# 32 stores of an intermediate tensor issued from GpSimd's queue instead of SyncE's, with a new instruction order

## The chip, the cores and the metric

The kernel runs on one NeuronCore of a Trainium2 chip. The core has TensorE (PE: matrix products, with the weight loads listed apart as PEld), VectorE (DVE), ScalarE (ACT), GpSimd (POOL) and SyncE (SP, which here issues DMA transfers). Each engine works through its own queue in order, and semaphores order the engines among each other. The metric is device time in microseconds (us); lower is better.

## The reference: three layers in a row

All tensors are float32. Batch is 4, sequence 448, model width 768.

```python
scores = cap * tanh(q @ k.T / sqrt(64) / cap)          # 12 heads of 64, per batch
x      = softmax(scores) @ v                            # layer 1: attention
h      = relu(x @ w_in)                                 # layer 2: 768 -> 1024 ("inner layer")
gate   = sigmoid(conv3(h, conv_w))                      # 3 taps along the sequence, per channel
x      = (h * gate) @ w_out                             # 1024 -> 768
for e in range(4):                                      # layer 3: 4 causal attention experts
    ye = softmax(mask(x @ wq[e] @ (x @ wk[e]).T / 8)) @ (x @ wv[e]) @ wo[e]
    out += w[e] * ye                                    # w: top-2 gate of x @ w_gate
```

## The kernel before

**Work.** The kernel folds `w_out` into the projections of layer 3 (`fold_w`, `fold_mm`), so layer 2 ends with the 8 blocks g = h * gate of 128 channels by 448 positions for each batch b. Products of float32 precision are made as three products of split operands. The stages overlap: attention of batch b + 1 runs while the inner layer of batch b is computed (`f_unit`), then come the fold, and layer 3 batch by batch.

**The values of the inner layer.** `f_unit(b, f, ...)` (L874) makes one block: matmuls into a PSUM bank, then a relu by ACT or DVE into h, which comes from the ring HT of 2 buffers. Where f < EARLY_N[b], with EARLY_N = (0, 4, 8, 0), the convolution and the gate follow at once (`conv_gate`, L898) into a buffer of the ring CT, also 2 buffers; otherwise h itself is stored and the gate is made later. The block is then stored to the DRAM tensor g_dram (L896), 224 KB at a time, 32 stores in all: 12 from CT (four of batch 1 and all eight of batch 2) and 20 from HT. `prep_g` and `prep_x` load the blocks back when layer 3 of that batch needs them. A store must have landed before its ring buffer is written again, and before its block is loaded.

**Order.** `chain_kernel` adds 2,487 operations to a `Plan`, which numbers them. They are then issued in the sequence of the tuple ORDER, written out in the source, so that each engine's queue follows it:

```python
for n in ORDER:
    for call in self.ops[n].calls:
        call()
```

The set SWAP names operations (copies, scalings, relus, absolute values) that run on the other one of ACT and DVE than the code says by default (`one_of`, L293). Each `add` states a cost, and HOP states a time between engines ("dma" 1500 ns plus size, "pool" 150 ns); no code here makes ORDER or SWAP out of them, they stand in the file as numbers.

**DMA.** Every transfer is issued by SP at L390 with a stated cost of 470 ns. POOL does memsets and selects only (L404); most stand at the start.

Of the kernel before, what the change touches and what calls it, by code (L numbers as in the profile page):

```python
# [201 lines left out]
class Plan:  # L202
# [192 lines left out]
    def store(self, out, in_, **kw):  # L395
        self.dma(out, in_, sb_in=in_, size=128 * self.cols(in_) * 4, **kw)
# [67 lines left out]
def chain_kernel(tc, first, kq, v, w_in, conv_w, woT, wqkv, wo, out):  # L464
    nc = tc.nc
    pl = Plan(nc)
# [5 lines left out]
    g_dram = tc.dram_tile([B, 128, NF, S], F32, name="g_dram")  # L472
# [401 lines left out]
    def f_unit(b, f, part, n, ring, pos, lag):  # L874
# [16 lines left out]
        g = h[:, 1:S + 1]  # L891
        if f < EARLY_N[b]:
            g = CT.next()
# [613 lines left out]
```

## Time and profile before

| | |
|---|---|
| time, median of 3 runs | 517.42 us (517.18 to 517.43) |
| the profiled execution's own time | 515.46 us |
| its span, first to last instruction | 513.8 us |
| outside the span | 1.66 us |
| TensorE clock granted in the span | 1.00, so 2.4 GHz |
| PE / DVE / ACT / POOL busy | 505.6 / 455.7 / 383.7 / 10.7 us |
| stores to g_dram | issued from 73.6 to 277.4 us |

"Busy" is the time in which an engine executes at least one instruction. The profiled execution is 1.96 us shorter than the median of the runs, so sums are made against 515.46 us and carried over to the median as differences.

### The profile page before, as it was taken

Reading aid. Unit: us, or ns where it says so; the run is one execution under the profiler, and the core shown is the slowest. Engines: PE = TensorE matmul, PEld = TensorE weight load, DVE = VectorE, ACT = ScalarE, POOL = GpSimd, SP = SyncE. Lnnn points to the kernel's source line nnn. Section 1 sums busy time; section 2 is a strip of 40 time slices with the busy share of each in tenths; the row PEclk is TensorE's granted clock in tenths of the full one; section 3 lists DMA queues with packets and bytes.
Section 4 is the critical chain, followed back from the end, with each engine's and each line's share of the span. In section 5 each row is a group of like instructions: output and inputs, shape, how many; then the busy total and the mean of one; then the engine's idle time right before and its main releaser. Section 6 shows DMA issues by size and latency. Waiting matters only on the chain.

```text
span 513.8 us, 9272 instructions
## 1 busy us (share of the span) xinstructions
PE 505.6 (98%) x3248; PEld 401.6 (78%) x3248; DVE 455.7 (89%) x1071; ACT 383.7 (75%) x689; POOL 10.7 (2%) x64
## 2 busy tenths in 40 slices
PE   9999999999999999999999999999999999999997
PEld 6344597555675576879999999999998998899886
DVE  5999999989998899798989999979879998997863
ACT  7999958999999989548534765577877777757771
POOL 4000000000000000010000000001000000000000
PEclk9999999999999999999999999999999999999999
DMA  6635346337531721465566251143577358507964
GB/s 211 194 133 184 129 155 201 122 112 185 159 104 46 199 93 62 153 200 171 187 219 203 75 169 39 54 132 92 169 232 260 115 198 273 175 20 248 307 231 153
DMA packets 48830, 81.73 MB, mean 159 GB/s; under 512 B 7696, under 2 KB 32272, under 8 KB 48784
## 3 DMA queue, kind: packets, MB, share of 16 engines
q1 hardware_dynamic: 48784, 81.15, 50.3%
q8 instruction: 25, 0.41, 0.4%
q14 instruction: 21, 0.17, 0.1%
HBM read 54.54 MB, written 22.66 MB: 150 GB/s over the span
## 4 chain that ended last, share of the span: by engine, by line
PE 68%; DVE 18%; ACT 6%; DMA 4%; issue 3%; SPq 1%; DVEq 0%; ACTq 0%
PE ps L381 67%; DVE fm L323 12%; DVE rm L323 5%; ACT fm L315 5%; SPq L390 1%; DMA fm<-p_dram 1%; DMA fm<-woT 1%; DMA p_dram<-fm 1%; DMA fm<-kq 1%; ACT rm L315 1%; DMA g_dram<-fm 0%; PE ps L385 0%; DVE ps L323 0%; DVEq L323 0%; ACTq L315 0%
## 5 line engine op out<-in xcount | busy, mean ns | idle before, releaser
L381 PE MATMUL ps<-rm 128*128 128x448 f32 (+8 forms) x2280 | 391.8, 350 | 2.8 <-ACT fm L315 2.1
L381 PEld LDWEIGHTS ps<-rm 128*128 128x128 f32 (+1 forms) x2280 | 351.6, 187 | 44.8 <-ACT fm L315 10.2
L315 ACT ACTIVATE fm<-fm 128x448 f32<-128x448 f32 (+9 forms) x233 | 168.3, 751 | 41.8 <-DVE fm L323 27.5
L323 DVE SCALAR_TENSOR_TENSOR fm<-fm 128x448 f32<-128x448 f32 (+4 forms) x240 | 147.4, 632 | 10.4 <-ACT fm L315 7.6
L315 ACT ACTIVATE fm<-ps,fm 128x896 f32<-128x896 f32 (+4 forms) x142 | 110.3, 796 | 16.6 <-DVE fm L323 7.2
L381 PE MATMUL ps<-fm 128*64 128x448 f32 (+10 forms) x952 | 115.8, 444 | 2.3 <-DVE fm L583 1.1
L381 PEld LDWEIGHTS ps<-fm 128*64 128x64 f32 (+4 forms) x952 | 48.2, 135 | 63.9 <-issue 41.3
L323 DVE TENSOR_TENSOR rm<-fm,rm 128x448 fp32r<-128x448 f32 (+4 forms) x154 | 86.7, 583 | 4.3 <-ACT rm L315 3.2
L323 DVE TENSOR_TENSOR fm<-fm 64x448 f32<-64x448 f32 (+6 forms) x112 | 61.3, 551 | 3.9 <-ACT fm L315 1.7
L315 ACT ACTIVATE fm<-ps 128x448 f32<-128x448 f32 (+5 forms) x80 | 38.6, 491 | 29.0 <-PE ps L381 25.7
L315 ACT ACTIVATE rm<-fm 128x448 fp32r<-128x448 f32 (+6 forms) x78 | 41.7, 551 | 19.6 <-DVE fm L323 15.4
L323 DVE TENSOR_SCALAR fm<-fm 128x256 int32<-128x256 int32 (+11 forms) x127 | 38.8, 322 | 6.4 <-ACT fm L315 2.8
L315 ACT ACTIVATE rm<-ps 128x386 fp32r<-128x386 f32 (+3 forms) x49 | 20.2, 424 | 19.0 <-PE ps L381 18.8
L323 DVE CAST rm<-fm 128x384 fp32r<-128x384 f32 (+6 forms) x81 | 28.8, 366 | 1.6 <-DMA fm<-kq 0.6
L315 ACT ACTIVATE rm<-rm 64x448 fp32r<-64x448 f32 (+3 forms) x50 | 24.6, 506 | 0.6
L323 DVE COPY fm<-ps 128x448 f32<-128x448 f32 (+4 forms) x27 | 13.5, 516 | 9.3 <-PE ps L381 5.6
L323 DVE TENSOR_TENSOR rm<-ps,rm 128x386 fp32r<-128x386 f32 (+1 forms) x32 | 18.7, 586 | 2.6 <-ACT rm L315 2.3
L323 DVE STREAM_TRANSPOSE fm<-fm 128x512 f32<-128x512 f32 x28 | 18.5, 692 | 1.6 <-ACT fm L315 1.4
L323 DVE TENSOR_REDUCE fm<-ps 128x1 f32<-128x384 f32 (+1 forms) x24 | 13.8, 576 | 0.4
L350 DVE CUSTOM_DVE_ANT_0 ps<-ps,fm 128x256 f32<-128x256 f32 (+1 forms) x32 | 11.3, 363 | 1.2 <-PE ps L381 0.9
L404 POOL MEMSET fm<- 64x3 f32 (+12 forms) x44 | 5.3, 148 | 324.4 <-PE ps L381 214.8
L323 DVE TENSOR_TENSOR fm<-fm,rm 128x448 f32<-128x448 f32 x18 | 11.0, 619 | 0.4 <-ACT fm L315 0.2
(27 smaller groups left out, 76.0 us busy)
## 6 DMA issues: line engine op xcount, KB each, us to landing
g_dram<-fm SPq DMA_DIRECT2D x32, 224.0 KB, 2.7
fm<-g_dram SPq DMA_DIRECT2D x32, 224.0 KB, 2.9
p_dram<-fm SPq DMA_DIRECT2D x14, 512.0 KB, 3.4
fm<-p_dram SPq DMA_DIRECT2D x28, 256.0 KB, 4.5
fm<-w_in SPq DMA_DIRECT2D x24, 256.0 KB, 2.7
fm<-woT SPq DMA_DIRECT2D x16, 384.0 KB, 3.4
fm<-kq SPq DMA_DIRECT2D x23, 256.0 KB, 3.4
out<-fm SPq DMA_DIRECT2D x23, 224.0 KB, 2.1
```

Of the source, the lines that this page charges most:

```text
L315: return self.add("act", cost, [lambda: self.nc.scalar.activation(out, in_, func, **kw)], [out] + more, [in_] + ptr)
L323: return self.add("dve", cost, [lambda: f(out, *ins, **kw)], [out], aps)
L350: self.add("dve", cost, [lambda: self.nc.vector.tensor_tensor_reduce(x, x, mask, -1.0, 3.0e38, OP.add, OP.min, least)], [x, least], [x, mask])
L381: self.nc.tensor.matmul(out, a, b, start=start, stop=stop, **kw))
L390: self.add("dma", 470.0, [lambda: self.nc.sync.dma_start(out, in_)], outs, ins, size=size, **kw)
L404: self.add("pool", cost, [lambda: f(out, *ins, **kw)], [out], [x for x in list(ins) + [kw.get("in_")] if hasattr(x, "ap")])
```

## The change

The store of each block is added by a new function, which lets GpSimd issue the transfer and states a cost of 3000 ns on POOL; the size is not stated. All other transfers stay on SP.

```diff
+    def store_by_pool(self, out, in_, **kw):
+        self.add("pool", 3000.0, [lambda: self.nc.gpsimd.dma_start(out, in_)], [], [in_], **kw)
...
-        pl.store(g_dram[b, :, f], g, keys_out=[("g", b, f)])
+        pl.store_by_pool(g_dram[b, :, f], g, keys_out=[("g", b, f)])
...
 ORDER = tuple(map(int, '''
...
-118 173 142 184 204 110 129 193 206 174 111 144 194 157 207 180 177 112 232 47 217 176 252 316 233 210 253 113 181 145
...
 SWAP = frozenset(map(int, '''
-82 86 95 99 102 110 114 124 128 133 137 144 148 151 159 166 175 186 197 204 219 223 226 230 235 250 253 265 272 278
...
+64 82 86 95 99 102 110 114 124 128 133 137 144 148 151 159 166 175 186 201 204 219 223 226 230 235 250 253 265 272 288
```

ORDER and SWAP are new. Counted through the numbered operations: the first 135 of the 2,487 places of ORDER are as before. PE's 420 operations move by 1.2 places in PE's queue on average and by 11 at most. SWAP differs in 185 numbers, which put 100 operations from ACT to DVE and 85 from DVE to ACT. In POOL's queue four older operations, memsets and a select that make masks, now stand among the stores.

## Rows read from the trace of the kernel before

**Rows 1.** The page, first part: busy us, share of the span, instructions.

```profile
PE 505.6 (98%) x3248; PEld 401.6 (78%) x3248; DVE 455.7 (89%) x1071; ACT 383.7 (75%) x689; POOL 10.7 (2%) x64
```

**Rows 2.** Busy time by stretch (--windows): PE, PEld, DVE, ACT, POOL, clock, DMA.

```profile
64.00:128.00 64.00, 63.84 (x429) 41.57 (x431) 60.39 (x121) 55.36 (x72) 0.00 (x0) 1.00 0.52 156
128.00:192.00 64.00, 64.00 (x442) 41.54 (x436) 58.28 (x99) 59.06 (x70) 0.00 (x0) 1.00 0.42 121
192.00:256.00 64.00, 64.00 (x363) 51.00 (x360) 56.19 (x95) 42.00 (x66) 1.58 (x3) 1.00 0.49 152
256.00:320.00 64.00, 64.00 (x352) 62.70 (x351) 59.09 (x123) 34.10 (x69) 0.52 (x2) 1.00 0.46 145
```

**Rows 3.** The page's chain that ended last: shares by engine.

```profile
PE 68%; DVE 18%; ACT 6%; DMA 4%; issue 3%; SPq 1%; DVEq 0%; ACTq 0%
```

**Rows 4.** What SP's queue waited for, whole span: total us, times, longest.

```profile
SPq L390 <- DVE fm L323: 164.3, 72, 12.9
SPq L390 <- DVE rm L323: 66.8, 32, 8.8
SPq L390 <- PE ps L381: 62.0, 17, 12.2
SPq L390 <- ACT fm L315: 28.8, 24, 4.6
```

**Rows 5.** g_dram's transfers (--tile): issue ns min/median/max, then landing of all.

```profile
L390 SPq DMA_DIRECT2D g_dram<-fm x32: 319/330/597, 73.6 to 277.4; - x32
...
DMA to landing us min/median/max: 1.9/2.8/6.9
```

**Rows 6.** Waits that ended in 64 to 256 us: total us, times, longest.

```profile
PEld ps L381 <- ACT fm L315: 10.0, 25, 0.8
...
PEld ps L381 <- DVE fm L323: 4.9, 12, 0.7
...
ACT fm L315 <- DMA g_dram<-fm: 2.7, 3, 1.9
...
PEld ps L381 <- DVE rm L323: 1.7, 3, 0.7
PEld ps L381 <- ACT rm L315: 1.0, 2, 0.7
ACT rm L315 <- DMA fm<-wqkv: 1.2, 1, 1.2
ACT fm L315 <- DMA fm<-w_in: 0.8, 1, 0.8
DVE rm L323 <- DMA fm<-kq: 0.6, 1, 0.6
```

**Rows 7.** Timeline of SP and of ACT about one store: start us, us, engine.

```profile
245.26 0.33 SPq L390 DMA_DIRECT2D g_dram<-fm  x1
...
247.29 0.67 ACT L315 ACTIVATE fm<-fm 128x448 f32<-128x448 f32 x1 [1.89 <-DMA g_dram<-fm]
```

**Rows 8.** Groups of DVE by form, 64 to 280 us: count, busy us, mean ns.

```profile
L323 DVE TENSOR_TENSOR rm<-fm,rm 128x448 fp32r<-128x448 f32 x37 | 22.2, 619 | 0.2
...
L323 DVE CAST rm<-fm 128x448 fp32r<-128x448 f32 x19 | 7.3, 383 | 0.9 <-DMA fm<-kq 0.6 <-PE ps L381 0.3
...
L323 DVE COPY fm<-ps 128x448 f32<-128x448 f32 x6 | 3.6, 622 | 1.3 <-PE ps L381 1.3
```

**Rows 9.** Timeline of POOL and DVE about 222 us.

```profile
221.54 0.56 DVE L323 CAST rm<-fm 128x772 fp32r<-128x772 f32 x1
...
221.76 0.49 POOL L404 MEMSET fm<- 128x128 f32 x1 [214.80 <-PE ps L381]
...
222.31 0.94 POOL L404 TENSOR_SCALAR_AFFINE_SELECT fm<-fm 128x128 f32<-128x128 f32 x1
...
223.21 0.20 POOL L404 MEMSET fm<- 128x128 f32 x1
```

**Rows 10.** Groups of ACT by form, whole span: count, busy us, mean ns.

```profile
L315 ACT ACTIVATE fm<-ps 128x448 f32<-128x448 f32 x60 | 32.0, 540 | 24.8 <-PE ps L381 22.1 <-DVE fm L323 1.6 <-PE ps L385 0.4
L315 ACT ACTIVATE rm<-fm 128x448 fp32r<-128x448 f32 x42 | 23.4, 571 | 6.5 <-DVE fm L323 3.6 <-PE ps L381 2.9
```

205 rows, old and new, of tables (ORDER, SWAP) are left out of this document.

## The prediction

> **What bounds the kernel now.** I read the page's first part first. PE is busy for 505.6 of 513.8 us, DVE for 455.7, ACT for 383.7 and POOL for 10.7 [rows 1]. The reader is to see that only PE has almost no idle time, and that POOL has nearly all of its time free. Then I cut the span into stretches [rows 2]. The stores are issued from 73.6 to 277.4 us [rows 5], which is inside these four stretches. In each of them PE is busy for 63.84 to 64.00 of 64 us; in the last PEld is busy for 62.70 as well, so there the weight loads follow each other without a break. In the stretches from 64 to 256 PEld is busy for 41.5 to 51.0 only, so there the matmuls are sometimes held up by their operands although PE counts as busy. From 64 to 256 DVE works 60.39 + 58.28 + 56.19 = 174.9 of 192 us (91%) and ACT 55.36 + 59.06 + 42.00 = 156.4 (81%).
>
> The chain that ended last says the same: PE has 68% of it, DVE 18%, ACT 6%, all DMA together 4%, and SP's queue 1% [rows 3]. SP spends its time waiting: its four longest items alone sum to 164.3 + 66.8 + 62.0 + 28.8 = 321.9 us, all of them waits for compute engines that must first make or free something [rows 4]. So SP has spare issue time; the question is only whether its order delays something that others need.
>
> Who needs it is in the waits that ended from 64 to 256 us [rows 6]. Loads that came late cost ACT 1.2 + 0.8 us and DVE 0.6 us, and no matmul or weight load names a DMA among its releasers there. The landing of a store to g_dram, which frees the buffer, cost ACT 2.7 us in 3 waits. PE's weight loads waited for ACT 10.0 + 1.0 us in 27 waits and for DVE 4.9 + 1.7 us in 15 waits.
>
> **The change, part by part.**
>
> *SP loses 32 issues.* Each takes 0.33 us [rows 5], together 10.6 us, which lie beside the 321.9 us of waiting [rows 4]. What SP can also lose is blocking: a store at the head of its queue waits for ACT or DVE, and the loads behind it wait too. The loads that come late in the stretch cost 1.2 + 0.8 + 0.6 = 2.6 us on ACT and DVE [rows 6]. Bounds: 0 to -2.6 us. I take 0, because PE names no DMA in that list and PE sets the time. If the cover goes, it is a late load of weights or of the next pair of heads that shows, on DVE first.
>
> The Trainium skill (DMA: Bandwidth & Descriptors, "Issuing engines are not separate DMA queues") says that several issuing engines share the same 16 DMA engines, and that using more of them saves sequencer time alone. By it nothing but the 10.6 us of SP's time would change, and the time would stay; that is the rival "hidden anyway" below. The trace agrees as far as SP's time is spare.
>
> *POOL gains 32 issues.* No row shows a DMA issued by POOL. The nearest rows are POOL's own instructions over 128 partitions: 0.20 us for a memset and 0.94 us for a select [rows 9]. SP's 0.33 us is the lower bound. I take 0.94 us, the longer row, so as not to underrate what I cannot see. 32 times 0.94 is 30 us in the 204 us of the stores, so POOL has room.
>
> *What waits behind a store on POOL.* In order, a store that waits for its relu or gate holds up the stores behind it and the four mask operations. In the trace of before these four run on POOL from 221.76 us on or later [rows 9], and their readers come still later, in layer 3; so nobody waits for them. A store that is held up keeps its ring buffer occupied, and the next relu or gate waits.
>
> *Landing.* Transfers of g_dram land 1.9 to 6.9 us after issue, 2.8 in the median [rows 5]. A landing that is later by 0.94 - 0.33 = 0.6 us matters only where the buffer is written again at once. Pairing each store with the next operation on its buffer, 7 of the 32 buffers are rewritten within 0.6 us of the landing. One pair shows it: the store is issued at 245.26, and ACT, idle for 1.89 us, starts at 247.29 [rows 7]. So ACT and DVE lose at most 7 x 0.6 = 4.2 us together. Six of the seven lie after 192 us, where ACT is busy for 42.0 and 34.1 of 64 us and PE never idles [rows 2]. Bounds 0 and +4.2; I take +0.3, half of the one early case. If the cover goes, PE waits for a bank that a late relu has not read. The blocks themselves are loaded back tens of us later, so no load waits.
>
> *VectorE beside POOL.* Copies, casts and scalings of DVE from SBUF to SBUF take 383 ns for 448 columns, against 619 ns for a two-operand operation and 622 for a copy from PSUM [rows 8]. There are 73 such fast ones from 64 to 280 us. One of them shows POOL suffering: the memset of 128 x 128 that ran over the cast at 221.54 took 0.49 us, the same memset at 223.21, beside none, 0.20 [rows 9]. If the exclusion also works the other way, DVE waits for POOL. 73 fast operations in 216 us start 0.32 times in the 0.94 us of a store; 32 x 0.32 = 10 meetings at half of 0.94 us each give DVE 4.8 us more. Of the 42 waits of weight loads that ACT or DVE ended, 15 were ended by DVE [rows 6]; by that share 4.8 x 15 / 42 = 1.7 us reach PE. Bounds 0 (POOL alone waits) and +4.8 (all of it reaches PE). I take +1.7, because DVE is at 91% and feeds ACT as well.
>
> The Trainium skill (SBUF — State Buffer, "SBUF: two separate sides") states such an exclusion: GpSimd and a DVE operation in a two-port mode lock each other out of a shared port pair, and transfers issued from GpSimd need it to write their descriptors. It speaks against this change. The slow memset agrees with one direction of it; no row shows the other, nor a descriptor being written.
>
> *The new order and the new shares of ACT and DVE.* PE's own order hardly moves (1.2 places on average), and the number of its instructions stays. From 64 to 256 us SWAP puts 7 PSUM reads and 21 SBUF operations of a few hundred columns from ACT to DVE, and 4 and 13 back: net 3 x 0.62 + 8 x 0.38 = 4.9 us more on DVE [rows 8] and 3 x 0.54 + 8 x 0.57 = 6.2 us less on ACT [rows 10]. DVE would be busy for 179.8 of 192 us (94%), ACT for 150.2 (78%). Weighted by who ends PE's waits [rows 6], relief of ACT could give up to 6.2 x 27 / 42 = 4.0 us, and load on DVE take up to all 4.9. I take 0: the relief goes to the engine with more room, the load to the one with less, but PE waits more often for ACT. Smaller moves within the order can't be priced from rows, and I leave them inside these bounds.
>
> *Sum.* 0 + 0.3 + 1.7 + 0 = +2.0 us: 515.46 becomes 517.5 for the profiled execution, and the median 517.42 becomes 519.4 us (+0.4%).
>
> **The rivals.**
>
> *Faster: ACT's relief reaches PE.* PE's weight loads wait for ACT 11.0 us in the stretch and for DVE 6.6 [rows 6]. If the shift of work removes 4.0 us of the first, and DVE adds only the 1.7 us of my sum, the time is 517.42 - 4.0 + 1.7 = 515.1 us. Against it: DVE at 94%. It decides if the waits for ACT fall under 9 us while those for DVE stay under 8.
>
> *Hidden anyway.* Stores are off PE's path, landings are covered, DVE and POOL don't meet: 517.4 us, within 1 us. For it: no PE wait names a DMA, and the chain has 1% of SP [rows 3, 6]. Against it: every buffer ring has only 2 buffers, and 185 operations change engine.
>
> *Slower by more: DVE is held up in full.* The 4.8 us all reach PE, and the landings take 0.3: 517.42 + 5.1 = 522.5 us. For it: DVE is the second fullest engine and would be fuller. Against it: only one POOL instruction in the trace is seen beside a fast DVE operation, and there it was POOL that waited.
>
> **How the numbers follow.** Some 0.2%, 1.0 us, is what a measurement of this kernel tells from no change. My forecast of +2.0 us has a chance of 0.38, hidden anyway 0.23, faster 0.28, slower by more 0.11. So faster by over 0.2% has 0.28, within it 0.23, slower 0.49. Cases of both signs hold most of the chance: the forecast's own range is 518.5 to 521.0, and the range that holds the time 8 times in 10 reaches from 514.6, a little under the faster rival, to 522.6, the slower one.
>
> **What would show it.** Right: SP's g_dram rows are gone and POOL has 32 transfers; POOL busy grows by some 30 us, if the profile counts their issue as busy; PE stays near 505 us busy; DVE's busy time from 64 to 256 us rises to about 180 us or more; its casts of 448 columns average over 383 ns; PE's waits for DVE grow past 6.6 us. Wrong: casts at 383 ns and landings of stores under 3 us (then the DVE term and the landing term are 0); a PE that waits less for ACT with the time below 516.4 us; or new waits ahead of 64 us or after 330 us, where no store runs and which only the order can have made.

## The result and the profile after

| | before | after |
|---|---|---|
| time, median of the runs taken side by side | 517.18 us (515.54 to 517.43, 5 runs) | 523.05 us (521.51 to 528.99, 5 runs) |
| ratio, with its 95% interval | | 1.0121 (1.0094 to 1.0147), +6.2 us |
| profiled execution, and its span | 515.46 us, 513.8 us | 523.1 us, 521.4 us |

The change makes the kernel slower. The sign is as forecast, the size is not: the forecast was +2.0 us, and the time lies above the upper end of its range, 522.6 us.

The page of the kernel after, its first part, the chain that ended last, and the two queues of data transfers (packets, MB, share of 16 engines):

```profile
PE 507.3 (97%) x3248; PEld 402.1 (77%) x3248; DVE 462.5 (89%) x1086; ACT 376.8 (72%) x674; POOL 27.2 (5%) x96
...
q1 hardware_dynamic: 44176, 73.81, 46.2%
q0 software_dynamic: 2048, 7.34, 3.8%
...
PE 47%; issue 22%; DVE 13%; DMA 8%; ACT 7%; POOL 2%; SPq 1%; POOLq 0%; DVEq 0%; ACTq 0%
```

PE is busy 1.7 us longer than before [rows 1], DVE 6.8 us longer, ACT 6.9 us less. The 32 stores now form a queue of their own. In the chain, PE's share falls from 68% to 47%, DMA's rises from 4% to 8% and that of issue from 3% to 22% [rows 3]: from 171 to 286 us the chain now runs mostly along POOL's queue of stores, and ends there in a landing of 4.26 us. Where PE lost its time shows in the stretches of the kernel after (columns as in [rows 2]):

```profile
64.00:128.00 64.00, 63.94 (x417) 42.47 (x419) 61.00 (x124) 55.02 (x69) 3.93 (x7) 1.00 0.54 168
128.00:192.00 64.00, 63.93 (x452) 40.92 (x446) 60.80 (x105) 58.88 (x68) 1.62 (x3) 1.00 0.40 112
192.00:256.00 64.00, 62.18 (x352) 48.33 (x349) 54.87 (x92) 39.00 (x61) 8.09 (x16) 1.00 0.45 137
256.00:320.00 64.00, 62.97 (x341) 60.73 (x340) 59.13 (x123) 30.23 (x62) 5.65 (x11) 1.00 0.48 153
...
384.00:448.00 64.00, 61.62 (x429) 55.30 (x428) 57.36 (x172) 45.64 (x116) 0.00 (x0) 1.00 0.63 202
```

In [rows 2] PE was busy for all 64.00 us from 192 to 256 and from 256 to 320. Now it idles for 1.82 and 1.03 us there. The first of these two stretches holds 12 of the 32 stores, the second the last 10. From 384 to 448, where no store runs, it idles for 2.38 us; in the kernel before it did not:

```profile
384.00:448.00 64.00, 64.00 (x438) 57.38 (x437) 60.84 (x177) 48.41 (x124) 0.00 (x0) 1.00 0.63 209
```

The transfers of g_dram in the kernel after (issue min/median/max in ns, then who waited, in us and times, then landing; the last line is one of the waits of the whole span):

```profile
L399 POOL DMA_DIRECT2D g_dram<-fm x32: 539/539/691, 71.7 to 287.5; - x32
...
  ACT fm L315: 20.7, 10
  DVE fm L323: 1.9, 1
...
DMA to landing us min/median/max: 2.2/3.3/7.0
...
ACT fm L315 <- DMA g_dram<-fm: 14.3, 4, 4.4
```

An issue on POOL takes 0.54 us, at most 0.69. ACT waits 20.7 us for transfers of g_dram, late loads among them, against 5.5 before by the same view. The landings of stores alone make 14.3 us in 4 waits, against 2.7 us in 3 before. One such wait can be followed towards PE. First SP's part of the timeline of the kernel after, then that of the other engines (a row with x2 or more merges instructions that follow each other):

```profile
225.60 1.26 SPq L390 DMA_DIRECT2D rm<-r_dram  x2
```

```profile
226.99 0.54 POOL L399 DMA_DIRECT2D g_dram<-fm  x1 [1.83 <-DVE fm L323]
...
233.79 0.67 ACT L315 ACTIVATE fm<-fm 128x448 f32<-128x448 f32 x1 [2.36 <-DMA g_dram<-fm]
...
234.50 1.22 DVE L323 SCALAR_TENSOR_TENSOR fm<-fm 128x448 f32<-128x448 f32 x2 [1.46 <-ACT fm L315]
...
242.83 1.49 PE L381 MATMUL ps<-rm 128*128 128x448 f32 x6 [1.50 <-ACT fm L315]
```

SP issues two loads of r_dram from 225.60 us on. POOL issues the store of batch 2's block 1, which the expectations below call that of layer 2, at 226.99. ACT waits for its buffer, DVE waits for ACT, and 9 us on, PE stands still for 1.50 us until 242.83. DVE had itself waited 1.94 us, until 228.64, for the store before this one, so the stall cannot be put down to ACT's wait alone. The landing of this store in the kernel after, and of the same store in the kernel before, where it was issued at 228.78 us:

```profile
DMA to landing us min/median/max: 6.7/6.7/6.7
...
DMA to landing us min/median/max: 1.9/1.9/1.9
```

### The profile page after: what moved, and what is told of

Its sections match the earlier page's. It is cut to its first block, busy times and chain, and to the rows that moved or that the text cites. A ratio compares the mean times of both kernels' runs of the same rounds, so it can differ in the third digit from the quotient of the medians.

```text
span 521.4 us, 9293 instructions
## 1 busy us (share of the span) xinstructions
PE 507.3 (97%) x3248; PEld 402.1 (77%) x3248; DVE 462.5 (89%) x1086; ACT 376.8 (72%) x674; POOL 27.2 (5%) x96
## 4 chain that ended last, share of the span: by engine, by line
PE 47%; issue 22%; DVE 13%; DMA 8%; ACT 7%; POOL 2%; SPq 1%; POOLq 0%; DVEq 0%; ACTq 0%
PE ps L381 46%; DVE fm L323 9%; ACT fm L315 7%; DVE rm L323 3%; DMA fm<-p_dram 2%; POOL g_dram L399 2%; DMA p_dram<-fm 2%; DMA fm<-v_dram 1%; DMA g_dram<-fm 1%; DMA fm<-kq 1%; DMA fm<-g_dram 1%; SPq L390 1%; DMA fm<-w_in 1%; PE ps L385 0%; ACT rm L315 0%
## 5 line engine op out<-in xcount | busy, mean ns | idle before, releaser
L381 PEld LDWEIGHTS ps<-rm 128*128 128x128 f32 (+1 forms) x2280 | 351.7, 187 | 49.5 <-ACT fm L315 12.1
L315 ACT ACTIVATE fm<-fm 128x448 f32<-128x448 f32 (+8 forms) x218 | 161.5, 767 | 43.6 <-DVE fm L323 27.1
L323 DVE TENSOR_TENSOR rm<-fm,rm 128x448 fp32r<-128x448 f32 (+5 forms) x154 | 87.5, 583 | 4.3 <-ACT rm L315 3.1
L315 ACT ACTIVATE rm<-fm 128x448 fp32r<-128x448 f32 (+5 forms) x74 | 39.2, 542 | 18.6 <-DVE fm L323 17.4
L323 DVE TENSOR_SCALAR fm<-fm 128x256 f32<-128x256 f32 (+12 forms) x142 | 44.1, 324 | 8.8 <-ACT fm L315 3.1
L323 DVE CAST rm<-fm 128x384 fp32r<-128x384 f32 (+6 forms) x85 | 30.4, 367 | 1.1 <-DMA fm<-kq 0.4
L399 POOL DMA_DIRECT2D g_dram<-fm x32 | 17.5, 549 | 262.0 <-ACT fm L315 140.8
L315 ACT ACTIVATE rm<-rm 128x128 fp32r<-128x128 f32 (+3 forms) x53 | 26.1, 499 | 3.0 <-DVE rm L323 2.2
L323 DVE COPY fm<-ps 128x448 f32<-128x448 f32 (+3 forms) x24 | 12.7, 545 | 5.0 <-PE ps L381 3.7
L350 DVE CUSTOM_DVE_ANT_0 ps<-ps,fm 128x128 f32<-128x128 f32 (+1 forms) x32 | 11.3, 359 | 2.7 <-PE ps L381 2.6
```

The costliest lines, as they stand in the source:

```text
L315: return self.add("act", cost, [lambda: self.nc.scalar.activation(out, in_, func, **kw)], [out] + more, [in_] + ptr)
L323: return self.add("dve", cost, [lambda: f(out, *ins, **kw)], [out], aps)
L350: self.add("dve", cost, [lambda: self.nc.vector.tensor_tensor_reduce(x, x, mask, -1.0, 3.0e38, OP.add, OP.min, least)], [x, least], [x, mask])
L381: self.nc.tensor.matmul(out, a, b, start=start, stop=stop, **kw))
L399: self.add("pool", 3000.0, [lambda: self.nc.gpsimd.dma_start(out, in_)], [], [in_], **kw)
```

## The experiments

Five theories are tested. L: a store that lands late holds one of two ring buffers, so a gate or relu waits, and then PE. O: the new order costs by itself. P: POOL's transfers and the fast copies of DVE hold each other up. Q: transfers land in the order in which they are issued, so a store that SP no longer issues falls behind loads that SP is now free to issue early. G: transfers from GpSimd are late by themselves. (N in the expectations says that the landing is not what costs, but something else that the new queue delays.) P can be judged from the rows. The casts of 128x448 in the kernel after, from 64 to 280 us:

```profile
L323 DVE CAST rm<-fm 128x448 fp32r<-128x448 f32 x18 | 6.9, 386 | 0.2
```

They took 383 ns before [rows 8], and the issues on POOL stay at 539 to 691 ns beside a DVE that is busy for 86 to 95% of each stretch from 64 to 320 us. No row shows a cost by P.

**Each half alone.** pool_old_order is the kernel before with one line changed (and the new function); sp_new_order is the kernel after with that line changed back.

```diff
-        pl.store(g_dram[b, :, f], g, keys_out=[("g", b, f)])
+        pl.store_by_pool(g_dram[b, :, f], g, keys_out=[("g", b, f)])
```

> The stores by GpSimd as in the change, but ORDER and SWAP as before. Theory L (the queue costs: a store issued by GpSimd lands later, 3.4 us in the median against 2.7, the two-buffer rings come free later, ACT waits and then PE): slower by 2 to 5 us, 519 to 522 us, with ACT waiting for g_dram landings over 10 us in all (2.7 us before) and matmul gaps over 0.4 us between 210 and 290 us. Theory O (the new order costs, whoever issues the stores): 517 us, within 1 us of before. Theory P (GpSimd's descriptor work and VectorE's fast copies exclude each other): slower, and the casts of 448 columns take clearly over 383 ns.

> New ORDER and SWAP, but the 32 stores issued by SyncE. Theory L: 517 us, within 1 us of before. Theory O: 521 to 523 us, as the changed kernel. If both hold in part: 519 to 521 us, with the PE stalls at about 241 and 286 us gone and those at the loads of p_dram and v_dram (397, 437, 491 us in the changed kernel) still there.

Measured: pool_old_order 525.77 us, ratio 1.0173 (1.0153 to 1.0194); sp_new_order 530.51 us, 1.0261 (1.0236 to 1.0285). Both are slower than any figure that the theories had given. Each half costs more alone than both do together, so neither "the queue" nor "the order" is the whole cause: the new order wins back some 2.7 us of what GpSimd's stores cost in the old one, and it costs 13.5 us if SP must issue its stores. In sp_new_order the largest stall of PE behind the start-up lies ahead of 192 us:

```profile
134.33 0.87 PE L381 MATMUL ps<-rm 64*128 64x448 f32 x5 [3.30 <-DVE fm L323]
```

In pool_old_order one store makes the largest stall, the same store as in the kernel after. Its timeline of ACT, DVE, POOL and PE:

```profile
230.69 0.54 POOL L399 DMA_DIRECT2D g_dram<-fm  x1 [3.78 <-DVE fm L323]
...
237.03 0.45 DVE L323 TENSOR_SCALAR fm<-fm 128x448 f32<-128x448 f32 x1 [3.30 <-DMA g_dram<-fm]
...
240.10 0.58 ACT L315 ACTIVATE fm<-fm 128x448 f32<-128x448 f32 x1 [4.08 <-DVE fm L323]
...
241.90 4.46 PE L381 MATMUL ps<-rm 128*128 128x448 f32 x13 [2.67 <-ACT fm L315]
```

**Parts of the order.** new_head_pool takes the new order up to the last store and keeps the rest of the old one, with POOL; new_tail_sp does the reverse, with SP. SWAP goes along. The sources have the numbers written out; in short:

```diff
-ORDER = new
+ORDER = new[:1292] + [n for n in old if n not in new[:1292]]
...
-ORDER = old
+ORDER = old[:1245] + [n for n in new if n not in old[:1245]]
```

> Stores by GpSimd, the new order up to the last store (place 1292 of 2487), then the remaining operations in the order of before; SWAP likewise. If the loss lies where the stores are: 520 to 522 us, with the stalls at about 241 and 286 us and none over 1 us at p_dram or v_dram loads after 380 us. If it lies in the order of layer 3: 517 to 518 us.

> Stores by SyncE, the order of before up to the last store (place 1245), then the remaining operations in the new order; SWAP likewise. If the new order of layer 3 costs by itself (late v_dram and p_dram loads on SyncE's queue): 519 to 521 us with PE stalls over 1 us at those loads. If it costs only after a late head: 517 us.

Measured: 526.19 us, 1.0173 (1.0149 to 1.0197), and 522.29 us, 1.0112 (1.0088 to 1.0136). These two tell little, and both are slower than expected. In both the largest stall comes some time behind the last store, where the two orders are joined (1.85 us, until 315.3 us, 26 us behind it in the first; 3.28 us, until 290.1 us, 12 us behind it in the second), and neither whole order has one of that size there. That the joint makes them is likely, not shown. They are not used below.

**Wider rings.** If L holds, more buffers must remove the cost and leave the landings as late as they are. The gates of batch 2 rotate over three buffers, and each relu of batch 3 has its own (the expectations say layer 2 and layer 3); the space was dead at that time. The batches 0 and 1 keep two.

```diff
+    HX = [fm.take(S + 2, at_) for at_ in [*range(14976, 14976 + 7 * 512, 512), 19072]]
+    CX = CT.bufs + [fm.take(S, 4800)]
...
-        h = HT.next()
+        h = HX[f] if b == 3 else HT.next()
...
-            g = CT.next()
+            g = CX[f % 3] if b == 2 else CT.next()
```

> Stores by GpSimd in the order of before, but the gates of layer 2 rotate over three buffers instead of two and each relu of layer 3 has a buffer of its own, so that from 215 to 290 us no relu of layer 3 waits for a landing and a gate waits for the third last one. Theory L (a late landing holds a ring buffer, ACT or DVE waits for it, then PE): the stall of PE of 2.83 us at 238.9 us and the fall of the granted clock behind it are gone, ACT's 14.7 us of waits for g_dram fall under 4 us, and the time is 517 to 519 us. Theory N (the landing is not what costs, the new queue delays something else, loads or the port of VectorE): the time stays at 524 to 527 us.

> The kernel before with the same wider rings, stores by SyncE. Theory L: PE hardly waits for a landing in the kernel before, so the time stays within 1 us of 517 us (at most 0.5 us is won). Theory N: the same, 517 us. If it gains more than 1 us, landings cost the kernel before something that its rows did not show.

> The changed kernel (stores by GpSimd, new order) with the wider rings: three buffers for the gates of layer 2, one for each relu of layer 3. Theory L (landings hold buffers): the four stalls of PE at 241.0, 246.4, 285.8 and 289.8 us, 3.5 us together, and the fall of the clock behind them are gone: 518.5 to 520 us. What is left over the 517 us of before is theory O's: the three late loads near 397, 437 and 491 us, 4.1 us of stall against 1.5 before. If the new order were the cause by itself the time would stay at 522 us or above.

> The new order with stores by SyncE and the wider rings; with two buffers this order cost 530.5 us. Theory L: the landings behind late loads hold no buffer that is needed, so most of the 13.7 us go and the time is 517 to 521 us. Theory O (in this order SyncE's queue itself is late, since a store waits 10 to 19 us at its head and the loads behind it wait too): 523 us or above.

| ratio to the kernel before | two buffers | wider rings |
|---|---|---|
| old order, SP | 1 | 0.9990 (0.9975 to 1.0005) |
| old order, POOL | 1.0173 (1.0153 to 1.0194) | 1.0021 (1.0006 to 1.0035) |
| new order, POOL (the change) | 1.0121 (1.0094 to 1.0147) | 1.0037 (1.0016 to 1.0058) |
| new order, SP | 1.0261 (1.0236 to 1.0285) | 1.0145 (1.0111 to 1.0179) |

The medians with wider rings are 516.73, 518.26, 519.94 and 524.96 us. Buffers take back 15.2 of the 17.3 thousandths in the old order, and 8.4 of the 12.1 in the new, which is 7.9 and 4.3 us. The second figure has an error of about 1.7 us by the two intervals, and by the medians it is 3.1 us. The landings themselves are as late as ever: 2.2/3.2/7.6 us in pool_old_order, and in pool_old_rings as the last row here shows; only less is waited for them (the 14.7 us of ACT's waits for transfers of g_dram in pool_old_order became 5.0, of which 1.4 are for a store):

```profile
  ACT fm L315: 5.0, 4
  DVE fm L323: 1.5, 1
...
DMA to landing us min/median/max: 2.2/3.2/8.0
```

In after_rings PE is without a gap again where the last stores are, and as late as in the changed kernel after 384 us (stretches, columns as in [rows 2]):

```profile
192.00:256.00 64.00, 64.00 (x360) 50.48 (x357) 56.50 (x96) 38.80 (x60) 8.68 (x17) 1.00 0.46 141
256.00:320.00 64.00, 64.00 (x351) 62.58 (x350) 60.99 (x128) 32.02 (x64) 6.51 (x14) 1.00 0.50 156
384.00:448.00 64.00, 61.95 (x428) 55.64 (x427) 57.55 (x172) 47.14 (x119) 0.00 (x0) 1.00 0.56 186
```

That execution took 518.26 us; the nine runs of after_rings lie in two groups, 516.8 to 518.3 and 519.9 to 520.5 us, and what parts them stays open.

L holds: the same buffers change nothing where the stores are SP's in the old order, and take most of the cost away where they are GpSimd's. O holds for the new order with SP, which keeps 1.0145. Why is open. The expectation speaks of stores that wait 10 to 19 us at the head of SP's queue; in the trace of sp_new_order no store is issued more than 6.0 us after SP's issue before it. In sp_new_rings the largest stall, 2.86 us until 134.1 us, comes behind a DVE that had waited 2.7 us for a load of kq. With POOL, the order's own share (1.0037 beside 1.0021) lies inside the intervals. sp_old_rings is within the noise of the kernel before, and no version here is faster.

**One store, and its place in line.** The store of batch 2's block 1 is tried in four ways. old_one_store_pool moves it alone to GpSimd, old_one_store_act moves it to ScalarE, sp_loads_first leaves it on SyncE but puts three loads ahead of it, and pool_old_sp_gate has all 32 on GpSimd, with a transfer of 64 numbers on SyncE at each store's old place. The lines of the edits follow in this order; the numbers are a part of ORDER, in which 1134, 1100 and 1099 are the loads.

```diff
+        (pl.store_by_pool if (b, f) == (2, 1) else pl.store)(g_dram[b, :, f], g, keys_out=[("g", b, f)])
...
+        self.add("act", 100.0, [lambda: self.nc.scalar.dma_start(out, in_)], [], [in_], **kw)
...
-911 923 905 906 1107 1113 934 1134 912 1100
+911 923 905 1134 1100 1099 906 1107 1113 934 912
...
+        self.add("pool", 3000.0, [lambda: self.nc.sync.dma_start(*first), lambda: self.nc.gpsimd.dma_start(out, in_)], [], [in_], **kw)
```

> The kernel before with a single store moved to GpSimd, that of layer 2's block 1 (issued at 228.78 us, landing after 1.94 us). Theory L with Q: this one lands after some 6 us behind the loads, DVE and ACT wait, PE stalls by 2 to 3 us near 238 us and its clock falls behind it: 520 to 523 us, so half or more of what all 32 cost. Rival (many small costs of 32 stores add up): at most 1 us more than before, 517 to 518 us.

> The kernel before, all stores by SyncE, but the three loads that followed the store of layer 2's block 1 in the queue (of wqkv and two of r_dram) are put ahead of it. Theory Q (what counts is whether the store goes out ahead of the loads or behind them): this store, issued at about 228.8 us by SyncE, lands after 5 to 7 us instead of 1.94 us, PE stalls by about 3 us near 237 us, 519 to 521 us, as with this one store on GpSimd. Theory G (transfers of GpSimd are late by themselves): it lands within 3 us and the time stays at 517 us.

> The kernel before with the one store of layer 2's block 1 issued by ScalarE. Theory Q: any queue but SyncE's sets the three loads free to go ahead, so the store lands after some 6 us, PE stalls by about 3 us near 237 us, 519 to 521 us. Theory G: it lands within 3 us, 517 us.

> Stores by GpSimd in the order of before; in addition SyncE issues, at each store's old place in its queue, a transfer of 64 numbers of one partition of the same block to a spare tensor, so that its loads again wait behind the relu or gate as before. Theory Q (a store by SyncE goes out ahead of the loads queued behind it, a store by GpSimd behind the loads that SyncE is now free to issue early): the store of layer 2's block 1 lands again within 2.2 to 2.6 us instead of 6.25 us, the stall of 2.83 us at 238.9 us is gone, the time is 518 to 520 us. Theory G (transfers issued by GpSimd land later by themselves): that store still lands after 4 us or more, and the time stays at 524 us or above.

| | ratio | this store: issued, landed after |
|---|---|---|
| old_one_store_pool | 1.0049 (1.0033 to 1.0064), 519.84 us | 228.9 us, 6.2 us |
| sp_loads_first | 1.0079 (1.0061 to 1.0098), 520.99 us | 228.5 us, 6.1 us |
| old_one_store_act | 1.0051 (1.0034 to 1.0068), 519.77 us | 230.4 us, 4.4 us |
| pool_old_sp_gate | 1.0149 (1.0124 to 1.0175), 525.06 us | 229.6 us, 4.3 us |

One store of 32 costs 2.5 us on GpSimd, 2.6 us on ScalarE, and 4.1 us on SyncE behind the loads; why most on SyncE was not followed. The expectation for old_one_store_pool, half or more of what all 32 cost, was missed: it is 2.5 of 8.9 us. The other 31 stores make the rest, and none of them was tried alone. SP's timeline of sp_loads_first (the last row merges this store and the next one, 8.69 us later), the row of this store, and the landings of the two loads of r_dram ahead of it:

```profile
225.07 1.37 SPq L390 DMA_DIRECT2D fm<-wqkv  x2
226.50 1.24 SPq L390 DMA_DIRECT2D rm<-r_dram  x2
228.51 9.02 SPq L390 DMA_DIRECT2D g_dram<-fm  x2
```

```profile
L390 SPq DMA_DIRECT2D g_dram<-fm x1: 332/332/332, 228.5 to 228.5; - x1
...
DMA to landing us min/median/max: 6.1/6.1/6.1
...
DMA to landing us min/median/max: 6.4/6.7/7.0
```

The timeline and the store's row of old_one_store_pool, where SP issues the same loads at once because no store stands in its way:

```profile
224.75 1.37 SPq L390 DMA_DIRECT2D fm<-wqkv  x2
226.17 1.24 SPq L390 DMA_DIRECT2D rm<-r_dram  x2
```

```profile
L399 POOL DMA_DIRECT2D g_dram<-fm x1: 693/693/693, 228.9 to 228.9; - x1
...
DMA to landing us min/median/max: 6.2/6.2/6.2
```

The store's row of old_one_store_act:

```profile
L399 ACTq DMA_DIRECT2D g_dram<-fm x1: 344/344/344, 230.4 to 230.4; - x1
...
DMA to landing us min/median/max: 4.4/4.4/4.4
```

And SP's timeline of the kernel before, where the store is at the head of the queue, holds up the loads, and goes out first:

```profile
228.78 0.33 SPq L390 DMA_DIRECT2D g_dram<-fm  x1
229.20 0.38 SPq L390 DMA_DIRECT2D fm<-wqkv  x1
229.64 1.24 SPq L390 DMA_DIRECT2D rm<-r_dram  x2
```

Behind the loads the store lands at 228.85 + 6.2 = 235.1 us from GpSimd, at 228.51 + 6.1 = 234.6 from SyncE and at 230.35 + 4.4 = 234.8 from ScalarE: each time 0.4 to 0.5 us after the last of the loads, which lands at 234.6, 234.2 and 234.3 us (worked out from the traces). In the kernel before the store lands at 230.7 us and the last of these loads at 235.8. So Q holds for this store, and its late landing needs no G: behind the loads SyncE's store is as late as GpSimd's.

But pool_old_sp_gate came out as G had said, and the remedy that Q suggested fails. SP waits for the gate again, and issues its loads at 229.71 and 230.09 us, right beside POOL's store of 229.64, which still lands after 4.3 us. So a start 0.07 us ahead of the loads did not give GpSimd's store its old place, as a start 0.42 us ahead gave it to SyncE's. Whether the small lead or GpSimd's way of issuing makes this difference was not separated. The stall near 238 us shrinks to 0.98 us, and a worse one, 4.19 us, appears at 291.8 us.

## Why the prediction was wrong, step by step

**SP's blocking (0, bounds 0 to -2.6 us): the step that failed.** The prediction saw that a store at the head of SP's queue makes the loads behind it wait, and took the end of that for a gain or nothing. It did not ask what the freed loads would then do. They go out ahead of the store, and the store waits for them. In the trace of the kernel after, the three loads issued from 225.22 to 226.28 us have landed by 233.24, and the store issued at 226.99 lands at 233.71 (worked out from the trace). This was tried for one store of 32; that it makes the other late landings too is not shown. So the bound should have reached far into the loss, and the rivals should have held this mechanism.

**Landing (+0.3, bounds 0 to +4.2): mis-sized by the same step.** "Later by 0.6 us" was right for a store that meets nothing: 2.2 us at the least on POOL against 1.9 on SP, and 0.3 us more from the end of the gate or relu to the issue (0.30 against 0.03 us, medians of the 26 and 20 stores whose releaser the trace tells). That was luck, since it had been worked out from the lengths of other instructions, and not from these two delays. In the median all landings are 0.5 us later (3.3 against 2.8 [rows 5]). Beside loads the lateness was 4.3 us, 6.2 against 1.9, and 4.8 us in the changed kernel. Together landings cost 7.9 us in the old order and 4.3 us in the changed kernel, by the rings, where the sum had 0.3.

**The cover.** The prediction counted on ACT's free time after 192 us and on a PE that never idles [rows 2]. A PE that never idles says that what feeds it has been in time, not by how much; here ACT's wait of 2.36 us and DVE's of 1.94 us end in 1.50 us on PE, which is gone with wider rings. "If the cover goes" was named, but the sum took 0.3 us for it.

**POOL's issue (0.94 us taken, 0.33 to 0.94):** 0.54 us, inside the bounds. POOL's busy time grew by 16.5 us, not by some 30.

**DVE beside POOL (+1.7, 0 to +4.8):** nothing of it shows. The casts took 386 ns against 383, as the prediction named for its own refutation. PE's weight loads waited less for DVE, not more (2.7 + 0.4 us from 64 to 256, against 6.6 [rows 6]), and for ACT about as long (11.9 + 0.3 against 11.0). The rival "slower by more", 522.5 us, came closest to the time, but by this term, which is not there.

**The new order (0, -4.0 to +4.9).** DVE's busy time from 64 to 256 us came to 176.7 us (179.8 forecast), ACT's to 152.9 (150.2). The order cannot be priced alone: it is worth some 2.7 us if GpSimd issues the stores and costs 13.5 if SP does. What is left of the change with wider rings is +1.9 us (0.8 to 3.0); the queue alone leaves 1.1 in the old order. Part of it may be late loads after 380 us, where the prediction said that only the order can make waits. These waits of the kernel after ended from 320 to 521 us:

```profile
PE ps L381 <- DMA fm<-p_dram: 2.5, 2, 1.3
PEld ps L381 <- DMA fm<-p_dram: 1.8, 2, 1.6
PEld ps L381 <- DMA fm<-v_dram: 1.5, 1, 1.5
...
PE ps L381 <- DMA fm<-v_dram: 1.1, 1, 1.1
```

Before, PE waited 0.7 us for p_dram there, its weight loads 0.3, and neither for v_dram; in after_rings PE waits 1.7 us for p_dram. Not all of this is the order's: a stall for p_dram near 490 us, 1.25 us in the kernel after and 0.67 before, is 1.31 us in sp_old_rings and 1.68 in old_one_store_act, which have the old order. Why these loads come late was not tried, and stays open.

**The rule of the Trainium skill** that the transfers of several issuing engines run on the same transfer engines (DMA: Bandwidth & Descriptors, "Issuing engines are not separate DMA queues") agrees with the three landings at 234.6 to 235.1 us. What the prediction drew from it, that the time would then stay, does not follow: moving an issue changes who goes first.

## What to carry to other kernels

A store that waits at the head of an in-order queue also holds back the loads behind it, and thereby keeps its own place in line; before moving it to another engine, list the loads that this sets free and ask whether its buffer is wanted again before they have landed. Where it is, add a buffer first: it removed most of the cost here where GpSimd issued the stores (15.2 of 17.3 thousandths, and 8.4 of 12.1), and 11.6 of 26.1 where SyncE issued them in the new order. And an order that comes with one queue is not neutral for another: measure the new queue and the new order each alone, since here each costs more than both.

## What the hardware showed that was not expected

Stores from three engines landed within half a microsecond of each other behind the same loads, at 234.6, 234.8 and 235.1 us, although they had been issued up to 1.8 us apart.

A stall of PE can cost more than its length. The stretches of pool_old_order about its stall (columns as in [rows 2]):

```profile
239.00:242.00 3.00, 0.33 (x3) 0.10 (x1) 1.62 (x3) 1.90 (x4) 0.54 (x1) 1.00 0.20 76
242.00:245.00 3.00, 3.00 (x10) 2.69 (x11) 3.00 (x6) 2.17 (x5) 0.00 (x0) 0.62 0.41 121
245.00:248.00 3.00, 3.00 (x13) 2.70 (x13) 2.88 (x6) 2.96 (x6) 0.54 (x1) 0.81 0.03 10
248.00:251.00 3.00, 3.00 (x17) 2.72 (x16) 2.90 (x7) 2.59 (x5) 0.37 (x1) 1.00 0.49 133
```

PE stood still for 2.67 us, and in the two stretches behind it the granted clock was 0.62 and 0.81, a mixture of the levels 1.2 and 2.4 GHz. That is 3 x (0.38 + 0.19) = 1.7 us of work on top, by estimate. The runs' mean granted clocks agree: 0.993 to 0.997 in the five of pool_old_order, 0.994 to 1.000 in the five of the change, 0.998 to 1.000 in the twelve of pool_old_rings. The mean of the first is 0.994, and 0.6% of 525 us is some 3 us (an estimate), a third of what GpSimd's stores cost there. In the kernel after, behind the stall of 1.50 us at 241.3, it stayed at 1.00:

```profile
241.00:244.00 3.00, 1.50 (x8) 1.09 (x7) 3.00 (x7) 2.62 (x6) 0.47 (x2) 1.00 0.72 207
244.00:247.00 3.00, 2.75 (x14) 2.21 (x12) 3.00 (x6) 2.94 (x6) 0.00 (x0) 1.00 0.33 132
```
